# Scheduler inputs, batch 1's mask, output buffers and a rounded layout changed in a fused attention and FFN kernel

## The chip, the cores and the metric

One core of one Trainium2 chip runs the program. The metric is device time in microseconds (us), the median over several executions. Engines are named as the profile names them: PE is TensorE's matmul, PEld its weight load, DVE is VectorE, ACT is ScalarE, POOL is GpSimd, SP is SyncE.

## The reference

Attention over 8 batches and 8 heads of 576 positions with 64 dimensions: heads 0 to 3 look at the last 32 positions, heads 4 to 7 at every fourth position of the last 128. Its output, laid out as 4608 tokens of 512, goes through a multiplicative feed-forward layer without a nonlinearity.

```python
scores = scale * np.matmul(q, k.transpose(0, 1, 3, 2))
mask_plain = (rel >= 0) & (rel < 32)
mask_dil = (rel >= 0) & (rel < 128) & (rel % 4 == 0)
scores = np.where(masks, scores, -1e9)
attn = np.exp(scores - max); attn = attn / attn.sum()
x = np.matmul(attn, v)               # (8, 8, 576, 64) -> (4608, 512)
a = x @ w1                           # w1, w2: 512 x 1024
b = x @ w2
h = a * b @ w3                       # w3: 1024 x 1024
out = h @ w_out                      # w_out: 1024 x 512
```

## The kernel before

**Attention.** In each batch, `u` = 0 is the four plain heads and `u` = 1 the four dilated ones, whose positions are taken residue by residue, so that both kinds need only a band of 128 keys for a block of 96 queries. A batch has 12 blocks (two `u` times six). q, k and v arrive by cast DMAs issued by GpSimd (`load_rows` L251, `load_v_plain` L288, `load_v_dil` L297); q and k of the very first half batch come unrounded over SyncE's queue into a staging area that is later `gt` (`load_whole` L260), and ScalarE rounds them in halves (`round_rows` L267). VectorE transposes q and k (`turn`, L401 and L416). A `Group` takes some blocks through scores (L467), the exponential on ScalarE (L478) and the mask. There are two ways to mask: in the first `BIASED` batches, groups hold three blocks and TensorE first adds a bias of -30000 outside the band by a product with the identity (L450); in the others groups hold `GRP` = 5 blocks, running on from batch to batch, and VectorE multiplies the exponentials by 0 or 1 (L486). That mask is made by five GpSimd instructions (L380), at the place that `MASK_AT` gives among GpSimd's DMAs. A `Step` is three blocks: the product with v and a column of ones (L509), reciprocal (L520) and normalisation (L523) on VectorE, and the transposition into `XT`: in the first two batches by TensorE (L537) with a copy out of PSUM by ScalarE (L545) or VectorE (L547), later by a DMA transpose on SyncE (L550). For the first two batches v's plain half is turned on TensorE too (L425, copies L435 and L437). `XT0` holds the plain heads, `XT1` the dilated ones.

**Feed-forward.** w3 and w_out are multiplied once into `wf_sb`: w3 is loaded (L336), transposed by VectorE (L659), multiplied with `wo_sb` (L679) and copied (L690 on ScalarE, L692 on VectorE). Tokens go in 16 units of 288, two per batch. `up` (L574) makes the products with w1 and w2, four matmuls for each 128 columns: two that read `XT1`, two that read `XT0`. ScalarE copies the first product (`copy_a` L585) and VectorE multiplies (`gate` L589) into `gt`. `down` (L600) multiplies tiles of 128 tokens with `wf_sb`; ScalarE copies the result into a buffer `osb` (L611), of which there are three, and SyncE stores it (L650). The last tile goes in two halves (`down_part` L618, `finish` L627), whose three pieces are copied into one `osb` tile.

**The order.** No hardware queue decides the order: `Plan` (L58 on) takes every step as a task with an engine, an assumed duration, dependencies and a priority, simulates the five engines, PSUM's eight banks and the stream of DMAs, and emits instructions in the order that comes out; each engine then runs its own list in that order, and real dependencies become semaphore waits. Priorities come from `FIRST` (batch 0) and `RANK` (others), the order of the first loads from `FIRST_LOADS`. `ON_DVE` names copies that VectorE does instead of ScalarE, `HALVED` those that both share. `SINGLE` is the number of products at the start that are made one 128-column piece at a time rather than two; `PARTED` is how many products of the first unit may be split into a part for the plain and one for the dilated heads. Where a load is issued the plan assumes (issue, transfer) times, and `BUSY` is added where a SyncE transpose is issued while the DMA stream is occupied. Where PE would idle before the first product, the plan inserts warming matmuls (L724; 25 more stand at the very start, L704).

Of the kernel before, what the change touches and what calls it, by code (L numbers as in the profile page):

```python
# [10 lines left out]
P = 128  # L11
BF16 = mybir.dt.bfloat16
# [17 lines left out]
BIASED = 2  # L30
LATE = False
W3_DVE = (0, 1, 2, 3)
SINGLE = 10
# [4 lines left out]
RANK = dict(E=14.678, VK=10.289, K=0.115, N=1.309, T=1.47, VT=1.262, S=3.624, V=0.444, X=8.99, W=0.183, C=2.862)  # L38
FIRST = dict(E=3.06, VK=0.542, K=2.149, N=1.723, T=5.596, VT=64.744, S=0.678, V=0.475, X=11.212)
WARM = 25  # L40
FILL = 110
FIRST_LOADS = ('k01', 'v00', 'q01', 'd0', 'v10', 'w0', 'w1', 'q10', 'k10', 'w2', 'q11', 'k11', 'd1', 'o0', 'o1', '33', '32', '31', '30')
SHIFT = {}
ON_DVE = ('VK0.0.1', 'VK0.1.1', 'VK1.0.0', 'VK1.1.0', 'W3D5', 'W3D6')
# [3 lines left out]
HALVED = ('K0.2', 'K0.3', 'VK0.1.0', 'VK0.1.1', 'VK1.0.0', 'VK1.1.0')  # L48
MASK_AT = 31.5
PARTED = 0  # L50
BUSY = 4500
# [14 lines left out]
class Plan:  # L66
# [15 lines left out]
    def run(self):  # L82
# [42 lines left out]
        while len(order) < n:  # L125
            progress = True
            while progress:
                progress = False
                for e in engines:
# [22 lines left out]
                    if e == "DMA":  # L152
                        free[e] = now + t.dur[0]
                        if t.dur[1]:
                            if len(landed) >= 8:
                                free[e] = max(now, landed[-8]) + t.dur[0]
                            dma = max(dma, free[e]) + t.dur[1]
                            t.end = dma + 1900
                            landed.append(t.end)
                        else:  # L160
                            t.end = free[e]
                    else:
                        t.end = free[e] = now + t.dur
                        if e == "SP" and t.name[0] == "X" and dma > now:
                            t.end = free[e] = now + t.dur + BUSY
                            dma += 1.5 * t.dur
# [23 lines left out]
def kernel(  # L190
# [60 lines left out]
    def load_rows(nm, src, b, us):  # L251
        if (nm, b) not in qk:
            qk[(nm, b)] = qk_pool.tile([P, 2, 18 * D], BF16, tag=nm, name=nm)
# [6 lines left out]
    def load_whole(nm, src, u):  # L260

        at = {"qn": 0, "kn": 18 * D, "vn": 36 * D}[nm]
# [4 lines left out]
    def round_rows(nm, u, half):  # L267

        at = {"qn": 0, "kn": 18 * D, "vn": 36 * D}[nm]
        if (nm, 0) not in qk:  # L270
            qk[(nm, 0)] = qk_pool.tile([P, 2, 18 * D], BF16, tag=nm, name=nm)
        o, i = qk[(nm, 0)][:, u, :], stage[:, at : at + 18 * D]
        if nm == "qn":
            n, c0 = ((5, 0), (4, 2 * D))[half]
            o, i = (
                bass.AP(tensor=x.tensor, offset=x.offset + c0, ap=[x.ap[0], [4 * D, n], [1, 2 * D]])
                for x in (o, i)
            )
        else:
            c = slice(9 * D * half, 9 * D * half + 9 * D)  # L280
            o, i = o[:, c], i[:, c]
        nc.scalar.copy(out=o, in_=i)  # L282
# [107 lines left out]
    def turn(b, u, nm, part):  # L390
# [6 lines left out]
        if part in (None, 6, 7):  # L397
# [5 lines left out]
        n, first, odd = ((5, 0, RUN + 4), (4, RUN, 5 - RUN))[part % 2]  # L403
        low = max(0, part // 2 - 1)
# [8 lines left out]
            offset=src.offset + (part % 2) * 64 + low * 32,  # L413
            ap=[src.ap[0], [128, n], [32, both], [1, 32]],
# [194 lines left out]
    def copy_y(i):  # L609
        o_sb = wk_pool.tile([P, d_model], F32, tag="osb", bufs=3, name="osb")  # L610
# [16 lines left out]
    def finish(i, half):  # L627

        if half == 0:
            held[("o", i)] = wk_pool.tile([P, d_model], F32, tag="osb", bufs=3, name="osb")  # L630
        o_sb = held[("o", i)]
# [4 lines left out]
        nc.vector.tensor_copy(out=o_sb[:, c0 : c0 + n], in_=held[("y", i, half)][:, 0:n])  # L636
        nc.sync.dma_start(out=rows[:, c0 : c0 + n], in_=o_sb[:, c0 : c0 + n])
        if half == 1:
            nc.scalar.copy(out=o_sb[:, c0 + n :], in_=held[("y", i, half)][:, n:])
            nc.scalar.dma_start(out=rows[:, c0 + n :], in_=o_sb[:, c0 + n :])  # L640
# [102 lines left out]
    def loads_rows(nm, b, us=None):  # L743
# [4 lines left out]
        t = load(f"L{nm}{b}", 700, 3100 if us is None else 1600, old,  # L748
# [4 lines left out]
    def loads_v(b):  # L753
        old = vdone.get((b - 2, 0), [])
        LV[(b, 0)] = [load(f"LP{b}", 1300, 4700, old, lambda: load_v_plain(b))]

    def loads_vd(b):
        old = vdone.get((b - 2, 1), [])
        LV[(b, 1)] = [
            load(f"LD{b}.{i}", 600, (800, 670, 400, 1070)[i], old, lambda i=i: load_v_dil(b, i))  # L760
# [5 lines left out]
    def loads_w12(c):  # L766
        return [
            load("LW", 800, (1700, 1700, 3300)[c], [], lambda d=d, s=s: load_w(d, s, WC[c]))
# [3 lines left out]
    for i, nm in enumerate(WHOLE):  # L772
        t = add(f"LF{nm}", "SP", 100, [], lambda nm=nm: load_whole(nm, rows_of[nm], 0), -9 + i,
                lat=4400 + 1350 * i)
        L[(nm, 0, 0)] = [
            add(f"C{nm}.{half}", "ACT", 650, [t], lambda nm=nm, h=half: round_rows(nm, 0, h),
                -9 + i + 0.1 * half, lat=100)
# [15 lines left out]
    for x in FIRST_LOADS:  # L793
# [3 lines left out]
        elif x[0] == "o":  # L797
            lwo[c] = load(f"LWO{c}", 600, 3300, [], lambda c=c: load_wo(c))
        elif x[0] == "3":
            n, move = (4, 700) if c in W3_DVE else (2, 1400)  # L800
# [38 lines left out]
    def turns(b, u, nm, pr):  # L839
# [4 lines left out]
        else:  # L844
            parts = (2, 3, 4, 5) if b == 0 else (0, 1)
# [16 lines left out]
    for b in range(B):  # L862
# [10 lines left out]
        if b < DIRECT_V:  # L873
            tv = turns(b, 0, "vn", 10 * b + rank("T", b))
            for half in range(2):
                x = add(f"VT{b}.0.{half}", "PE", 420, tv[half] + [idt],
# [61 lines left out]
        while steps < 4 * B:  # L938
# [21 lines left out]
            if bb < TURNED:  # L960
                x = add("X" + n, "PE", 310, ns + [idt], st.back, bb - 99 + rank("X", bb), slot=1)
# [10 lines left out]
            else:  # L972
                x = [add("XD" + n, "SP", 1300, ns, st.back_dma, 0, lat=1200)]
# [39 lines left out]
    def downs(i):  # L1013
# [4 lines left out]
        if i == n_y - 1:  # L1018
            for half in range(2):
# [3 lines left out]
                    after=stores[-3:-2])  # L1023
# [4 lines left out]
                 after=[stores[-3] if len(stores) > 2 else None])  # L1028
        stores.append(add("ST", "SP", 300, [cy], lambda: store(i), 0, lat=3000))
# [61 lines left out]
```

## Time and profile before

| | us |
|---|---|
| device time, four runs | 254.45, 255.04, 256.07, 257.23 |
| median | 255.55 |
| the profiled execution | 255.04 |
| its span | 253.3 |
| TensorE busy | 242.7 |
| VectorE busy | 158.5 |
| ScalarE busy | 109.5 |
| GpSimd busy | 62.4 |

How to read the rows: a group's row names the line, engine, operation, output <- input, shape and count, then the busy time, the mean in ns of one instruction, and the idle time in front of the group with what ended it. A timeline row has start, length, engine, line and, in brackets, the idle time before it. Matmuls overlap in the pipeline, so the price of one is read from the distance of starts, not from the mean length. In the page's slices each digit is tenths busy in a fortieth of the span. The rows that matter are shown with the prediction.

### The profile page before, as it was taken

What the parts mean: (1) busy time and instruction counts of PE and PEld (TensorE: products, weight loads), DVE (VectorE), ACT (ScalarE), POOL (GpSimd) and SP (SyncE); (2) the same over time, 40 slices, a digit from 0 to 9 for tenths busy, and PEclk for the clock granted to TensorE, in tenths of its full rate; (3) what the DMA queues carried; (4) which work ended last, traced back from release to release, by engine and by line L of the source; (5) the groups of instructions that cost most, each with busy time, mean ns of one, the idle gap of its engine ahead of it and who ended that gap; (6) DMA issues with size and microseconds to landing.
All of it is one profiled execution on the core that took longest, in us unless ns stands there. A gap on an engine that the chain in (4) does not pass through costs nothing.

```text
span 253.3 us, 6390 instructions
## 1 busy us (share of the span) xinstructions
PE 242.7 (96%) x2694; PEld 167.1 (66%) x2694; DVE 158.5 (63%) x270; ACT 109.5 (43%) x154; POOL 62.4 (25%) x96
## 2 busy tenths in 40 slices
PE   7799999999996999999999999999999999999994
PEld 5488677646555657667677676776766766777752
DVE  3988575879776797888488591974545543232221
ACT  5655555225513354452544523553535524323321
POOL 7754479378212223133002110300000000000000
PEclk9999999999999999999999999999999999999999
DMA  7999999999999999999994929294161631221114
GB/s 225 197 200 205 203 203 144 159 192 189 184 210 162 217 206 242 150 102 173 168 172 52 145 51 135 84 117 92 43 91 41 67 91 41 70 73 49 44 41 124
DMA packets 58749, 33.90 MB, mean 134 GB/s; under 512 B 42081, under 2 KB 49633, under 8 KB 58721
## 3 DMA queue, kind: packets, MB, share of 16 engines
q0 software_dynamic: 37920, 19.34, 60.0%
q1 hardware_dynamic: 20656, 14.10, 29.6%
q8 instruction: 21, 0.34, 0.6%
q10 hardware_dynamic: 144, 0.07, 0.1%
q14 instruction: 8, 0.06, 0.1%
HBM read 39.85 MB, written 9.44 MB: 195 GB/s over the span
## 4 chain that ended last, share of the span: by engine, by line
PE 77%; DMA 18%; ACT 1%; issue 1%; POOL 0%; DVE 0%; SPq 0%; ACTq 0%; POOLq 0%; DVEq 0%
PE ps L574 44%; PE ps L600 21%; PE ps L679 5%; DMA kn<-in_k_dram 5%; DMA out_dram<-osb 4%; PE ps L509 3%; DMA w_sb<-in_moe_w_dram 3%; PE ps L467 3%; DMA w3n<-in_moe_w_dram 3%; DMA vn<-in_v_dram 3%; ACT et L478 1%; PE ps L618 1%; DVE et L486 0%; ACT asb L585 0%; ACT osb L611 0%
## 5 line engine op out<-in xcount | busy, mean ns | idle before, releaser
L574 PE MATMUL ps<-XT,w_sb 128*128 128x288 bf16 x1024 | 135.9, 286 | 0.2 <-ACT asb L585 0.2
L574 PEld LDWEIGHTS <-w_sb 128*128 128x128 bf16 x1024 | 97.9, 98 | 30.5 <-issue 0.2
L589 DVE TENSOR_TENSOR gt<-ps,asb 128x576 bf16<-128x576 f32 (+1 forms) x69 | 49.2, 713 | 62.4 <-PE ps L574 56.6
L585 ACT CAST asb<-ps 128x576 bf16<-128x576 f32 (+1 forms) x69 | 41.7, 605 | 66.9 <-PE ps L574 65.2
L600 PE MATMUL ps<-wf_sb,gt 128*128 128x512 bf16 x280 | 65.7, 379 | 0.0
L600 PEld LDWEIGHTS <-gt 128*128 128x128 bf16 x280 | 27.0, 98 | 26.9
L611 ACT COPY osb<-ps 128x512 f32<-128x512 f32 x35 | 20.4, 587 | 51.0 <-PE ps L600 48.0
L478 ACT ACTIVATE et<-ps 128x1920 bf16<-128x1920 f32 (+2 forms) x23 | 34.4, 1510 | 5.6 <-PE ps L467 5.6
L301 POOL DMA_DIRECT2D vd<-in_v_dram x32 | 21.3, 671 | 48.8 <-PE ps L509 43.7
L523 DVE TENSOR_TENSOR xo<-ps,rcp 96x768 bf16<-96x768 f32 x32 | 30.1, 949 | 0.7
L416 DVE STREAM_TRANSPOSE qt<-qn 128x320 uint32<-128x320 uint32 (+3 forms) x34 | 22.2, 674 | 2.1 <-ACT qn L282 1.7
L486 DVE TENSOR_TENSOR et<-et,mask 128x960 bf16<-128x960 bf16 (+1 forms) x30 | 17.7, 630 | 0.3 <-ACT et L478 0.2
L509 PEld LDWEIGHTS <-et 128*128 128x128 bf16 x384 | 14.2, 98 | 2.9 <-ACT et L478 1.6
L467 PE MATMUL ps<-qt,kt 32*128 32x96 bf16 x768 | 12.5, 201 | 3.5 <-ACT osb L611 2.1
L520 DVE RECIPROCAL rcp<-ps 96x12 f32<-96x12 f32 x32 | 6.7, 217 | 14.5 <-PE ps L509 14.4
L467 PEld LDWEIGHTS <-kt 32*128 32x128 bf16 x768 | 9.2, 92 | 9.2 <-issue 7.2
L679 PE MATMUL ps<-wo_sb,w3T 128*128 128x512 bf16 x64 | 14.1, 379 | 0.0
L416 DVE STREAM_TRANSPOSE kt<-kn 128x320 uint32<-128x320 uint32 (+3 forms) x18 | 11.4, 641 | 2.5 <-PE ps L467 2.3
L290 POOL DMA_DIRECT2D vp<-in_v_dram x6 | 7.2, 1200 | 22.1 <-PE ps L509 16.1
L336 POOL DMA_DIRECT2D w3n<-in_moe_w_dram x16 | 9.3, 585 | 7.7 <-DVE w3T L659 4.3
L679 PEld LDWEIGHTS <-w3T 128*128 128x128 bf16 x64 | 6.3, 98 | 7.2
L401 DVE STREAM_TRANSPOSE kt<-kn 128x576 uint32<-128x576 uint32 (+1 forms) x9 | 10.0, 1123 | 0.5 <-PE ps L467 0.5
(56 smaller groups left out, 112.7 us busy)
## 6 DMA issues: line engine op xcount, KB each, us to landing
qn<-in_q_dram POOLq DMA_DIRECT2D x6, 576.0 KB, 9.6
kn<-in_k_dram POOLq DMA_DIRECT2D x6, 576.0 KB, 11.4
w3n<-in_moe_w_dram POOLq DMA_DIRECT2D x16, 128.0 KB, 6.6
out_dram<-osb SPq DMA_DIRECT2D x7, 256.0 KB, 2.3
out_dram<-osb SPq DMA_DIRECT2D x8, 224.0 KB, 3.4
vp<-in_v_dram POOLq DMA_DIRECT2D x6, 288.0 KB, 11.1
out_dram<-osb SPq DMA_DIRECT2D x8, 192.0 KB, 2.3
out_dram<-osb SPq DMA_DIRECT2D x8, 160.0 KB, 2.7
```

The lines of the kernel that those rows point to most:

```text
L301: nc.gpsimd.dma_start(out=vds[b % 2][p0 : p0 + n, :, mu, 16 : 16 + 2 * D], in_=v_rows(b, 4, 4 * t0 + res, [[4 * D, n], [S * D, 4], [1, 2 * ...
L416: nc.vector.transpose(out=o, in_=i)
L467: nc.tensor.matmul(out=self.sp[:, g, QB * i : QB * i + QB], lhsT=kt[prt, u, QB * m : QB * m + P, c], rhs=qq, start=(c == 0 and not biased) ...
L478: nc.scalar.activation(out=ev, in_=self.sp[:, :, 0:x], func=ACT.Exp, scale=scale)
L509: nc.tensor.matmul(out=self.o[:, g, mm, :], lhsT=grp.et[:, c0 : c0 + P], rhs=vv, start=True, stop=True,)
L523: nc.vector.tensor_tensor(out=self.xo[0:QB, :].rearrange("p (m g d) -> p g m d", m=3, g=4), in0=self.o[0:QB, :, :, self.val : self.val + D ...
L574: nc.tensor.matmul(out=o[:, i, :], lhsT={"a": w1_sb, "b": w2_sb}[key][:, c, f * P : (f + 1) * P], rhs=unit_cols(k, c), start=(first and j ...
L585: nc.scalar.copy(out=held[("s", k, fs[0])], in_=held[("a", k, fs[0])])
L589: nc.vector.tensor_tensor(out=gt[:, fs[0] : fs[-1] + 1, c0 : c0 + UNIT], in0=held[("b", k, fs[0])], in1=held[("s", k, fs[0])], op=AL.mult,)
L600: nc.tensor.matmul(out=y, lhsT=gt[:, f, c0 : c0 + P], rhs=wf_sb[:, f, :], start=(f == 0), stop=(f == KFF - 1),)
L611: nc.scalar.copy(out=o_sb, in_=held[("y", i)])
L679: nc.tensor.matmul(out=o, lhsT=w3T[ft][:, g // 2, :, g % 2] if ft // 2 in W3_DVE else w3T[ft][:, g, :], rhs=wo_sb[:, g, :], start=(g == 0) ...
```

## The change

The plan's assumed times for transfers, transposes and stores are replaced by others, with a different rule for SyncE while DMA is busy, and the priorities, load order and assignment of copies are other numbers; with these the plan gives another order on every engine. `BIASED` falls from 2 to 1, so batch 1's blocks join the groups of five that VectorE masks, and the last of these groups with blocks of batch 1 runs on into batch 2. `MASK_AT` puts the mask's five instructions ahead of all loads that are still to be issued. `SINGLE` = -132 makes every product two pieces wide, `PARTED` = 80 lets all products of unit 0 be parted. `osb` has six buffers, and the last tile's three pieces get a buffer each. The first q's rounded halves are stored one behind the other instead of interleaved, and `turn` reads them so; v's tile for rows holds one half batch.

```diff
-BIASED = 2
+BIASED = 1
+OSB = 6
+QUARTERS = ('qn', 'kn')
-SINGLE = 10
+SINGLE = -132
-RANK = dict(E=14.678, VK=10.289, K=0.115, N=1.309, T=1.47, VT=1.262, S=3.624, V=0.444, X=8.99, W=0.183, C=2.862)
-FIRST = dict(E=3.06, VK=0.542, K=2.149, N=1.723, T=5.596, VT=64.744, S=0.678, V=0.475, X=11.212)
+RANK = dict(E=0.351, VK=60.432, K=24.778, N=0.18, T=72.284, VT=18.559, S=28.466, V=10.21, X=6.94, W=1.028, C=33.53)
+FIRST = dict(E=0.125, VK=3.069, K=21.212, N=0.305, T=7.654, VT=0.231, S=160.797, V=2.276, X=20.076)
-FIRST_LOADS = ('k01', 'v00', 'q01', 'd0', 'v10', 'w0', 'w1', 'q10', 'k10', 'w2', 'q11', 'k11', 'd1', 'o0', 'o1', '33', '32', '31', '30')
+FIRST_LOADS = ('v00', 'k01', 'q01', 'q10', 'v10', 'd0', 'w1', 'w0', 'k10', 'q11', 'k11', 'w2', 'd1', 'o0', '32', 'o1', '31', '30', '33')
-ON_DVE = ('VK0.0.1', 'VK0.1.1', 'VK1.0.0', 'VK1.1.0', 'W3D5', 'W3D6')
+ON_DVE = ('K0.0', 'K0.2', 'K0.3', 'K1.0', 'K1.1', 'K1.2', 'VK1.1.0', 'VK1.1.1', 'W3D3', 'W3D5', 'W3D7')
-HALVED = ('K0.2', 'K0.3', 'VK0.1.0', 'VK0.1.1', 'VK1.0.0', 'VK1.1.0')
-MASK_AT = 31.5
-PARTED = 0
-BUSY = 4500
+HALVED = ('K0.2', 'K1.0', 'K1.3', 'VK1.0.1', 'VK1.1.0', 'VK1.1.1')
+MASK_AT = -61.5
+PARTED = 80
+BUSY = 7500
...
-                        if e == "SP" and t.name[0] == "X" and dma > now:
-                            t.end = free[e] = now + t.dur + BUSY
-                            dma += 1.5 * t.dur
+                        if e == "SP" and now > 20000 and dma > now:
+                            t.end += min(BUSY, dma - now)
+                            dma += (1.5 if t.name[0] == "X" else 1) * t.dur
...
-        o, i = qk[(nm, 0)][:, u, :], stage[:, at : at + 18 * D]
+        o, i = qk[(nm, 0)][:, 0, :], stage[:, at : at + 18 * D]
         if nm == "qn":
             n, c0 = ((5, 0), (4, 2 * D))[half]
-            o, i = (
-                bass.AP(tensor=x.tensor, offset=x.offset + c0, ap=[x.ap[0], [4 * D, n], [1, 2 * D]])
-                for x in (o, i)
+            i = bass.AP(
+                tensor=i.tensor, offset=i.offset + c0, ap=[i.ap[0], [4 * D, n], [1, 2 * D]]
             )
+            o = o[:, 10 * D * half : 10 * D * half + n * 2 * D]
+            nc.scalar.copy(out=o.rearrange("p (n x) -> p n x", n=n), in_=i)
...
+        pitch, at = (64, 320) if (b, u, nm) == (0, 0, "qn") and nm in WHOLE else (128, 64)
...
-            offset=src.offset + (part % 2) * 64 + low * 32,
-            ap=[src.ap[0], [128, n], [32, both], [1, 32]],
+            offset=src.offset + (part % 2) * at + low * 32,
+            ap=[src.ap[0], [pitch, n], [32, both], [1, 32]],
...
-        o_sb = wk_pool.tile([P, d_model], F32, tag="osb", bufs=3, name="osb")
+        o_sb = wk_pool.tile([P, d_model], F32, tag="osb", bufs=OSB, name="osb")
...
-        if half == 0:
-            held[("o", i)] = wk_pool.tile([P, d_model], F32, tag="osb", bufs=3, name="osb")
-        o_sb = held[("o", i)]
...
-        nc.vector.tensor_copy(out=o_sb[:, c0 : c0 + n], in_=held[("y", i, half)][:, 0:n])
-        nc.sync.dma_start(out=rows[:, c0 : c0 + n], in_=o_sb[:, c0 : c0 + n])
+        y = held[("y", i, half)]
+        o_sb = wk_pool.tile([P, d_model], F32, tag="osb", bufs=OSB, name="osb")
+        nc.vector.tensor_copy(out=o_sb[:, 0:n], in_=y[:, 0:n])
+        nc.sync.dma_start(out=rows[:, c0 : c0 + n], in_=o_sb[:, 0:n])
         if half == 1:
-            nc.scalar.copy(out=o_sb[:, c0 + n :], in_=held[("y", i, half)][:, n:])
-            nc.scalar.dma_start(out=rows[:, c0 + n :], in_=o_sb[:, c0 + n :])
+            o2 = wk_pool.tile([P, d_model], F32, tag="osb", bufs=OSB, name="osb")
+            nc.scalar.copy(out=o2[:, 0:n], in_=y[:, n:])
+            nc.scalar.dma_start(out=rows[:, c0 + n :], in_=o2[:, 0:n])
...
-        t = load(f"L{nm}{b}", 700, 3100 if us is None else 1600, old,
+        t = load(f"L{nm}{b}", 700, 2850 if us is None else 1450, old,
...
-        LV[(b, 0)] = [load(f"LP{b}", 1300, 4700, old, lambda: load_v_plain(b))]
+        LV[(b, 0)] = [load(f"LP{b}", 1300, 1900, old, lambda: load_v_plain(b))]
...
-                x = [add("XD" + n, "SP", 1300, ns, st.back_dma, 0, lat=1200)]
+                x = [add("XD" + n, "SP", 1700, ns, st.back_dma, 0, lat=1200)]
...
-                 after=[stores[-3] if len(stores) > 2 else None])
-        stores.append(add("ST", "SP", 300, [cy], lambda: store(i), 0, lat=3000))
+                 after=[stores[-OSB] if len(stores) >= OSB else None])
+        stores.append(add("ST", "SP", 900, [cy], lambda: store(i), 0, lat=1500))
```

The other assumed times change in the same way (weights 1700 to 1400 and 3300 to 2580, w_out 3300 to 2500, w3 700 to 680, v's dilated parts, roundings, turns back).

## The prediction

> **What bounds the kernel now.** I read the page first, then the chain of waits in order of time, then TensorE's own timeline, then the groups of instructions by shape and the timelines of VectorE and GpSimd around the places that the change touches.
>
> ```profile
> PE 242.7 (96%) x2694; PEld 167.1 (66%) x2694; DVE 158.5 (63%) x270; ACT 109.5 (43%) x154; POOL 62.4 (25%) x96
> ...
> PE   7799999999996999999999999999999999999994
> ...
> PEclk9999999999999999999999999999999999999999
> DMA  7999999999999999999994929294161631221114
> ```
>
> TensorE is busy for 96% of the span at full granted clock; the only thin spots are the first slices and one after 75 us. The DMA engines are saturated for the first half.
>
> ```profile
> 43.04 4.90 PE ps L574 x40
> 47.94 10.36 PE ps L679 x48
> ...
> 69.98 10.28 DMA out_dram<-osb
> 80.34 0.59 ACT osb L611
> 80.98 0.61 PE ps L467 x40
> ...
> 247.82 1.76 PE ps L618 x16
> ```
>
> This is the chain of waits (start, length, what). From 43.04 on it is one TensorE matmul after another, with one excursion: a store of the output (10.28 us from issue to landing, at 69.98) releases ScalarE's copy out of PSUM at 80.34, and that releases score matmuls at 80.98. So a microsecond of TensorE work or waiting is a microsecond of time.
>
> ```profile
> 18.86 0.50 PE L425 MATMUL ps<-ident,vt 128*128 128x128 bf16 x6
> 19.19 1.63 PE L574 MATMUL ps<-XT,w_sb 128*128 128x288 bf16 x12
> ...
> 42.87 5.07 PE L574 MATMUL ps<-XT,w_sb 128*128 128x288 bf16 x40
> ...
> 80.98 0.61 PE L467 MATMUL ps<-qt,kt 32*128 32x96 bf16 x40 [2.06 <-ACT osb L611]
> ```
>
> TensorE's own timeline (start, length, line, shape, count, idle before): the first w1/w2 product (L574) starts at 19.19, and the store costs 2.06 us of idle time.
>
> The time as a sum. The steps between chain rows give a price for one matmul: L574 0.1225 us (4.90/40), 512 columns 0.2158 (10.36/48), a score 0.014 (0.56/40), L509 0.0305 (0.73/24), L537 0.045 (0.26/6), L425 0.06, L618 0.11. With the page's counts: 1024 L574 125.4, 280 L600 60.4, 64 L679 13.8, 16 L618 1.8, 384 L509 11.7, 768 L467 10.7, 32 L450 3.9, 48 L537 2.2, 24 L425 1.4: 231.3 us of work. At 43.04 the work ahead of it in the queue adds up to 28.8, so 14.2 had gone to waiting and warming matmuls. From there to 249.58 pass 206.5 us for 202.5 of work: 4.0 lost, 2.2 of it at the store, the rest some 0.1 after each score group. The tail to 253.30 is 3.7. 14.2 + 231.3 + 4.0 + 3.7 = 253.2, the span. The profiled execution took 255.04, 1.74 more than its span; the median of the runs shown is 255.55, 0.5 above it.
>
> **The change part by part.**
>
> ```profile
> L486 DVE TENSOR_TENSOR et<-et,mask 128x960 bf16<-128x960 bf16 x28 | 17.1, 650 | 0.3 <-ACT et L478 0.2
> ...
> L450 PE MATMUL ps<-bias,ident 128*128 128x288 bf16 x32 | 5.3, 287 | 0.0
> ```
>
> *Batch 1 masked by VectorE.* Its four groups of three blocks lose their 16 bias matmuls (L450): 16 x 0.1225 = 1.96 us of TensorE work, and the built order has 21 score groups instead of 23, 0.1 each: **-2.1 us**. VectorE's order gains four multiplications of 0.650 us, two of 768 columns (0.348 to 0.650, I take 0.53) and loses two of 0.348: +3.0 us. VectorE is busy 39.8 of the first 55 us, and has gaps of 2.7 us at 27, 36.6 and 43, so I cost that at nothing on the path; without that cover it is at most 3.0. ScalarE's exponentials stay (8 x 1.128 + 14 x 1.777 + 0.816 against 4 x 1.128 + 16 x 1.777 + about 1.46, 34.7 and 34.4).
>
> *Six osb buffers.* The copy at 80.34 is the fourth; its product was done at 75.8, and it waited for the first store, landed at 80.26. With six buffers that store is needed by the seventh copy, which this trace has at 92.7: **-2.2 us**. Bound: 0 if something else holds ScalarE there; nothing else is named. In the final tile each part has a buffer of its own:
>
> ```profile
> 249.60 0.29 DVE L636 COPY osb<-ps 128x128 f32<-128x128 f32 x1 [0.45 <-PE ps L618]
> 249.97 0.27 ACT L639 COPY osb<-ps 128x128 f32<-128x128 f32 x1 [1.49 <-DVE osb L636]
> ```
>
> In these rows of the end ScalarE's last copy waits for VectorE's copy into the same tile, though its product ended at 249.58: it starts 0.35 earlier, and its transfer is the last issued: **-0.3 us** (0 to -0.35).
>
> *First q's rounded halves apart.*
>
> ```profile
> 6.08 1.46 DVE L416 STREAM_TRANSPOSE qt<-qn 128x320 uint32<-128x320 uint32 x2 [1.75 <-ACT qn L282]
> 7.40 1.23 DVE L401 STREAM_TRANSPOSE kt<-kn 128x288 uint32<-128x288 uint32 x2
> ```
>
> VectorE's first transposition waits for both roundings on ScalarE (4.81 + 0.725 + 0.612, overlapping, end 6.05). Apart, it starts after the first, at 5.6. Of the 0.45 us nothing reaches the scores, because of the next part.
>
> *The order.* This is the large unknown. VectorE's queue now has v's transposition (1.24 us) and two of k's quarter pieces ahead of the second half of the first k. GpSimd issues v before k now; the first two such loads landed at 7.54 and 9.0, so k's quarters wait for 9.0. The queue: q 5.6 to 6.95, half of k to 7.6, v to 8.85, quarters 9.05 to 9.85, k's other half to 10.5. The first scores start at 10.6 instead of 8.68. Behind them VectorE still has six quarters and batch 1's first q (to 13.5), then two steps of reciprocal and normalisation at 0.22 + 0.95 less overlap (15.75), a copy of XT (576 wide; 288 took 0.308, so 0.31 to 0.62, I take 0.46), half a q and batch 1's v (17.95), two more steps (20.2). L540 turns the last, and the first L577 starts at **20.6**, where 19.19 was. The four w1/w2 quarters must have landed: two of them now go behind batch 1's q (1.4 us), all behind the masks.
>
> ```profile
> 35.79 4.76 POOL L380 TENSOR_SCALAR mask<-bias 128x384 bf16<-128x384 bf16 x5
> ```
>
> GpSimd's five mask instructions, 4.76 us, stood at 35.79 and now stand at about 5.1, in front of v, vd and the weights. This is covered by the transfers already queued: landings follow each other by 1.3 to 1.5 us per 288 KB (7.54, 9.0, 10.35), so the two loads of q end at 11.8, and a load issued at 9.85 lands 3.9 later (0.57 of issue, then about the 3.0 of the quickest w3n load, and half a us for its size), 13.7 instead of 13.2. Then vd (2.2 us, from its landings), weights at 1.2 each: 17.0, 18.2, 19.4, 20.7, just in time. [...]
>
> From the first L577 to the point where both first units are done (128 of them) there are 18.7 us of work in the new order; before, 21.8 took 23.85. I follow the queue: a short wait for the gate in front of batch 1's scores (0.3), one for normalisation in front of the first turn back (0.5), 0.2 for the rest, that is 40.3. As before lost 2.05 there, I take 1.7: **41.0**. Bounds: 39.7 (waits of 0.4) and 44 (kn and qn of batch 1, by the same steps at 22.1 and 23.5, each 1.5 late, and the second w_out load, at 39.4, after the 40 us at which the fused weights need it).
>
> In the new order 26.0 us of work lie ahead of that point (28.8 less 1.96 of bias, 0.86 for 16 scores, 12 L509 and 6 L537 that now come later), so 15.0 are lost there against 14.2: **+0.8 us**. From there 229.3 - 26.0 = 203.4 us of work remain and 1.8 of small losses: TensorE ends at 246.2. The mask's old place costs nothing any more: q and k of batch 2 landed at 52.1 and 54.8, now some 4.5 earlier. Tail 3.4, outside the span 1.74: **251.35 on the profiled execution, 3.7 less (the parts, -2.1 - 2.2 - 0.3 + 0.8, give 3.8); on the median 251.8.** Of the rest (larger PSUM-to-SBUF copies by VectorE instead of ScalarE, double units from the start, eight fused-weight copies shared 3 to 5) each moves below a microsecond between engines with gaps, and I cost it at 0.
>
> **The rivals.**
> 1. *The masks aren't covered.* If the queue runs dry for most of the 4.76 us, weights and batch 1's k land up to 3 us later, and the first unit and all behind it with them: 254 to 255. For it: the four weights land without margin. Against: landings that follow the transfers by 1.4 us each show a backlog until 11.8.
> 2. *Slower: batch 1's last scores hang on batch 2's loads.* Its third group holds two blocks of batch 1 and three of batch 2, so TensorE, which takes its queue in order, stands there (at about 54) until batch 2's q and k have landed and been transposed (1.3 us after k). I have k at 50.4, margin 2. If it lands at 52.6 it begins to cost, one for one; the gain is gone at 56.3, and over 1% is lost from 58.9 on: 259. Before, it landed at 54.8 behind the masks, so it needs four microseconds worse than that.
> 3. *The store's wait only moves.* VectorE's later transpositions or batch 2's DMA transposes (up to 12 us to landing at 75 to 100, needed at about 87, issued at about 76) end in its place: 2.2 come back, 254.
>
> **How the numbers follow.** Forecast 0.60, rival 1 0.15, rival 3 0.13, rival 2 0.12. About 1% is what a measurement of this kernel tells from no change, 253.0 and 258.1. The forecast lies below 253.0 almost whole (0.58 of 0.60), and a few of the rivals 1 and 3 do (0.03); rival 2 is slower by over 1% in most of its 0.12. Faster 0.61, same 0.28, slower 0.11. The forecast's own range, from the bounds 39.7 and 42.5, is 250.3 to 253.3; with rivals 1 and 3 taken in, and 0.7 below for the small losses, 249.6 to 255.5.
>
> **What would show it.** L450 falls to 16 and the idle time before scores around 80 is gone; ScalarE's osb copies wait only for TensorE; the first L577 at 20.6 and the first L682 at 41; TensorE's end near 246; the last ScalarE copy starts with its product's end. Wrong would be a wait in front of L682 or the scores at 54 named after a DMA, w_sb named in front of the first L577, or score groups at 85 to 90 that wait for XT.

## The result and the profile after

The kernel after takes **256.06 us** (median of 53 runs, 253.6 to 261.95), the kernel before 254.49 (79 runs, beside them): ratio **1.0035, 95% interval 1.0021 to 1.005**. The ratio leaves out the executions in a second, slower state (12 of the 53), which the median of 256.06 contains. It is slower by 0.9 us on that ratio, where 3.7 less was forecast. The profiled execution took 255.45 with a span of 253.7.

The page of the kernel after: busy time by engine, then TensorE's 40 slices, its granted clock and the bytes moved.

```profile
PE 243.7 (96%) x2687; PEld 167.1 (66%) x2687; DVE 162.8 (64%) x274; ACT 106.2 (42%) x143; POOL 62.3 (25%) x96
...
PE   7895999999999999999999999999999999999994
...
PEclk9997999999999999999999999999999999999999
...
GB/s 226 183 141 204 202 199 200 188 169 187 197 161 214 196 158 216 227 220 179 112 125 83 84 136 78 151 44 65 90 44 90 44 65 90 46 70 52 41 44 124
```

A slice is 6.3 us. The hole after 75 us is gone; a new one is in the fourth slice, 19 to 25 us, where the granted clock sinks too, and the transfers run at 141 GB/s in the slice before it. The chain of waits (start, length, what) says what it is:

```profile
5.07 4.77 POOL mask L382 x5
10.36 2.66 POOL vd L303 x4
13.02 2.19 POOL w_sb L313 x3
15.21 9.19 DMA w_sb<-in_moe_w_dram
24.44 3.98 PE ps L577 x24
```

The end hangs on GpSimd's masks, on the issues of v's dilated loads and of the weights behind them, and on the fourth weight load, which took 9.19 us from issue to landing. The store at 69.98 and ScalarE's copy at 80.34 have left the chain. TensorE's timeline around it:

```profile
20.16 0.43 PE L540 MATMUL ps<-ident,xo 96*128 96x96 bf16 x6
23.23 5.67 PE L577 MATMUL ps<-XT,w_sb 128*128 128x288 bf16 x32 [2.63 <-DMA w_sb<-in_moe_w_dram]
...
44.77 3.62 PE L682 MATMUL ps<-wo_sb,w3T 128*128 128x512 bf16 x16
```

TensorE is through with the work ahead of the first up product at 20.59, as forecast (20.6). It then waits 2.63 us for weights, 32 products take 5.67 us, and the first fused-weight product starts at 44.77 instead of 41.0. From there to TensorE's end at 250.0 are 205.2 us, exactly the forecast's 203.4 + 1.8. So against the forecast 3.8 us are lost ahead of 44.77 and nothing behind it, up to TensorE's end.

The windows of the kernel after (stretch; busy time of the engines; then granted clock, DMA share, GB/s):

```profile
10.00:12.00 2.00, 2.00 (x56) 1.32 (x58) 1.93 (x6) 1.63 (x3) 2.00 (x4) 1.00 0.84 128
12.00:14.00 2.00, 1.74 (x54) 1.51 (x40) 1.92 (x6) 1.46 (x2) 2.00 (x4) 1.00 1.28 175
14.00:16.00 2.00, 1.41 (x41) 0.94 (x38) 1.97 (x5) 0.93 (x1) 2.00 (x4) 1.00 1.41 133
16.00:18.00 2.00, 2.00 (x52) 1.61 (x52) 1.96 (x4) 1.15 (x2) 2.00 (x4) 1.00 1.13 129
18.00:20.00 2.00, 2.00 (x38) 1.77 (x34) 1.87 (x3) 2.00 (x5) 0.78 (x2) 1.00 1.31 168
```

GpSimd (the fifth busy column) is occupied without a pause to 18, yet the transfers run at 128 to 175 GB/s, where the kernel before has 188 to 213 in these stretches. The four weight loads land at 19.3, 20.7, 23.2 and 24.4.

Theory A: GpSimd issues nothing for 4.77 us while it makes masks, the stream of transfers thins, and the weights come 3.7 us late (the prediction's rival 1). Rivals: the new order of the loads, or their mix, is the cause, whatever GpSimd does (B and F below); or the sunken clock is. In most of the experiments the plan's order is kept and only named tasks are emitted elsewhere, behind `order, _ = plan.run()`. Every ratio is to the kernel before, run beside it.

### The profile page after: what moved, and what is told of

Read it like the earlier page. It is cut to its first block, busy times and chain, and to the rows that moved or that the text cites. A ratio compares the mean times of both kernels' runs of the same rounds, so it can differ in the third digit from the quotient of the medians.

```text
span 253.7 us, 6352 instructions
## 1 busy us (share of the span) xinstructions
PE 243.7 (96%) x2687; PEld 167.1 (66%) x2687; DVE 162.8 (64%) x274; ACT 106.2 (42%) x143; POOL 62.3 (25%) x96
## 4 chain that ended last, share of the span: by engine, by line
PE 88%; POOL 5%; DMA 4%; DVE 1%; issue 1%; ACT 0%; POOLq 0%; ACTq 0%
PE ps L577 50%; PE ps L603 24%; PE ps L682 5%; PE ps L512 4%; PE ps L470 4%; DMA w_sb<-in_moe_w_dram 4%; POOL mask L382 2%; POOL vd L303 1%; POOL w_sb L313 1%; PE ps L621 1%; PE ps L540 0%; POOL qn L258 0%; POOL vn L258 0%; DVE xo L526 0%; ACT asb L588 0%
## 5 line engine op out<-in xcount | busy, mean ns | idle before, releaser
L577 PE MATMUL ps<-XT,w_sb 128*128 128x288 bf16 x1024 | 138.3, 288 | 2.9 <-DMA w_sb<-in_moe_w_dram 2.6
L592 DVE TENSOR_TENSOR gt<-ps,asb 128x576 bf16<-128x576 f32 x64 | 48.3, 754 | 59.9 <-PE ps L577 58.9
L588 ACT CAST asb<-ps 128x576 bf16<-128x576 f32 x64 | 40.9, 639 | 69.3 <-PE ps L577 67.8
L489 DVE TENSOR_TENSOR et<-et,mask 128x960 bf16<-128x960 bf16 (+1 forms) x34 | 20.5, 645 | 0.2 <-ACT et L481 0.2
```

Source lines behind the costliest of these rows:

```text
L489: nc.vector.tensor_tensor(out=ev, in0=ev, in1=mk, op=AL.mult)
L577: nc.tensor.matmul(out=o[:, i, :], lhsT={"a": w1_sb, "b": w2_sb}[key][:, c, f * P : (f + 1) * P], rhs=unit_cols(k, c), start=(first and j ...
L588: nc.scalar.copy(out=held[("s", k, fs[0])], in_=held[("a", k, fs[0])])
L592: nc.vector.tensor_tensor(out=gt[:, fs[0] : fs[-1] + 1, c0 : c0 + UNIT], in0=held[("b", k, fs[0])], in1=held[("s", k, fs[0])], op=AL.mult,)
```

## Experiments: where the masks stand

**Masks behind the four weight loads.** The kernel after, and:

```diff
     order, _ = plan.run()
+    moved = [t for t in order if t.name.startswith("masks")]
+    order = [t for t in order if not t.name.startswith("masks")]
+    at = [i for i, t in enumerate(order) if t.name == "LW"]
+    at = at[3] + 1
+    order[at:at] = moved
```

> The changed kernel, every list as it is but GpSimd's: the five mask instructions go behind the issue of the first four weight loads (w1 and w2, columns 0 to 511). Theory A (the masks keep GpSimd from issuing, the DMA stream runs thin from 10 to 18 us, and the weights land 3.7 us late): the fourth weight lands near 20.7 instead of 24.4, the first L577 starts at 20.2 to 20.7, the granted clock stays at 1.0 between 22 and 26 us, L682 starts near 41.5 instead of 44.77, and the time falls by 3 to 3.5 us, to some 252. Theory B (this mix of loads moves at 130 to 175 GB/s whoever issues it): the weights still land after 23, the time stays within 1 us of 255.5. Theory C (a wait at batch 1's scores takes its place, because batch 1's k is issued at 16 either way): the first product starts at 20.6, but the time falls by less than 2 us, with an idle time of over 1 us in front of the first scores of batch 1.

Measured: 254.14, ratio 0.9971 (0.9947 to 0.9995). Its TensorE timeline:

```profile
20.37 4.19 PE L577 MATMUL ps<-XT,w_sb 128*128 128x288 bf16 x32
...
40.85 3.62 PE L682 MATMUL ps<-wo_sb,w3T 128*128 128x512 bf16 x15
...
58.15 3.63 PE L682 MATMUL ps<-wo_sb,w3T 128*128 128x512 bf16 x15 [1.68 <-DVE w3T L662]
```

The wait for weights is gone and the fused weights start 3.9 earlier, as theory A says. But the masks (now at 14.18) hold up the loads behind them: the transfers fall to 138 GB/s at 20 to 22, VectorE waits for w3, and TensorE 1.68 for it at 58.15. TensorE ends at 248.68, 1.3 before the kernel after: 2.6 of the 3.9 are given back.

**Masks behind batch 1's k.** The same edit with `"Lkn1"` and `[1]`: three more loads go first.

> The same, with the masks one step further, behind batch 1's k and q as well, where GpSimd only waited for transfers. Theory A: the gain of the run before, and batch 1's k lands near 22 instead of 25.8, so no wait in front of batch 1's scores: 3.5 to 4.5 us faster than the changed kernel, 251 to 252. Theory B: within 1 us of 255.5. Theory C: this run, other than the one before it, brings the whole gain. If the masks come late for VectorE's first multiplication of batch 1 (at 28 to 30 us), an idle time of VectorE in front of L489 shows it; I expect none, as they end near 18.

Measured: **252.73, ratio 0.9915 (0.9887 to 0.9943)**. Masks at 15.86; the transfers stay at 195 to 213 GB/s from 14 to 26.

```profile
40.68 3.62 PE L682 MATMUL ps<-wo_sb,w3T 128*128 128x512 bf16 x15
...
56.00 3.63 PE L682 MATMUL ps<-wo_sb,w3T 128*128 128x512 bf16 x15 [0.23 <-DVE w3T L662]
...
89.15 5.07 PE L577 MATMUL ps<-XT,w_sb 128*128 128x288 bf16 x40 [0.73 <-DMA XT<-xo]
```

One move of five instructions is worth 3.3 us on the medians, and the kernel is then faster than both. The 0.73 at 89.15 is the prediction's rival 3 in small: a DMA transposition comes too late.

**The converse: masks early in the kernel before.** The same loop, its insertion point ahead of the first `LD0` load. The masks are then made from the bias tile before its blocks are filled, so later batches are multiplied by other masks.

> The kernel before, with its own order, in which only the five mask instructions of GpSimd are emitted earlier, ahead of the first dilated load of v, as in the kernel after. Theory A (masks in front of the loads thin the stream of transfers and delay the first weights): the weights, which land at 15.8, 17.0, 18.6 and 19.7 in the kernel before, land 3 to 4.5 us later, at 19 to 24; the DMA rate at 10 to 18 us falls from about 200 GB/s to 130 to 180; the first fused-weight matmul (L679) comes 2 to 4 us after 43.04; the time rises by 1.5 to 4 us, to a ratio of 1.006 to 1.016. Rival B (the order of the loads of the kernel after is what costs, not the masks): weights within 1 us of before, time within 0.7 us of before.

Measured: 258.33, ratio 1.0145 (1.0096 to 1.0194). (The 43.04 quoted there is the start of the 40 up products ahead of the fused weights; their first, L679, stands at 47.77 in the kernel before.)

```profile
23.39 1.63 PE L574 MATMUL ps<-XT,w_sb 128*128 128x288 bf16 x12
...
51.98 4.26 PE L679 MATMUL ps<-wo_sb,w3T 128*128 128x512 bf16 x19
...
84.10 0.61 PE L467 MATMUL ps<-qt,kt 32*128 32x96 bf16 x40 [0.99 <-ACT osb L611]
```

The first up product, 19.19 before, and the first fused weight both come 4.2 later; the wait for the store, 2.06 before, shrinks to 0.99, as TensorE arrives later. 4.2 - 1.07 = 3.1 is the growth of the span, 253.3 to 256.4.

The weights do come late: GpSimd's next issues, which wait for the four of them, start at 19.40, 21.40, 22.99 and 24.02 instead of 16.08, 17.30, 18.91 and 19.94, and the transfers run at 75 to 155 GB/s from 10 to 18. But this is not what makes the time. Here the masks read the bias tile ahead of VectorE's last write to it, so that write waits for them, and with it the first transposition (6.08 before). VectorE's timeline, then TensorE's first scores (8.68 before):

```profile
9.40 0.22 DVE L373 MEMSET bias<- 32x192 bf16 x1 [6.25 <-POOL mask L380]
9.55 1.38 DVE L416 STREAM_TRANSPOSE qt<-qn 128x320 uint32<-128x320 uint32 x2
```

```profile
12.07 0.67 PE L467 MATMUL ps<-qt,kt 32*128 32x96 bf16 x24 [1.75 <-DVE kt L401]
```

The write stands at 4.12 in the kernel before. 3.4 of the 4.2 are lost by the first scores, the rest while the granted clock is 0.53 and 0.62 (12 to 16), and at 23.39 TensorE waits for no weight. So the old order shows the late landings of theory A, but its time decides nothing between A and B. The next run does.

**Masks on VectorE.** The kernel after, its order untouched:

```diff
-        nc.gpsimd.tensor_scalar(
+        nc.vector.tensor_scalar(
```

> The kernel after with its order unchanged, in which the five mask instructions run on VectorE, where they stand between the last bias fill (to 4.36) and the first transposition (5.62, which waits for ScalarE), and GpSimd has no mask at all. Theory A (GpSimd's 4.76 us of masks in front of the loads is the whole fault): the second load of v is issued at 5.0, the four weights land between 15 and 20 (19.3 to 24.4 in the kernel after), the first up product starts at 20.2 to 20.6 without a later stop, the first fused-weight matmul at 40.5 to 41; and as GpSimd makes no masks later either, the later loads and the transposes of XT come no later than in masks_behind_k, so the time is that of masks_behind_k or up to 0.8 less: 251.9 to 252.7, ratio 0.989 to 0.9925. VectorE's masks take 0.9 to 1.4 us, and if they run past 5.62 the first scores move by that (0 to 0.3 us). Rival F (the order of the loads is at fault as well): weights later than 21, time 254 or more.

Measured: 253.27 (6 runs, 251.97 to 258.38), ratio 0.9926 (0.988 to 0.9972). The masks take 0.2 us each there; the first transposition starts at 5.65 instead of 5.62, the first up product at 20.48 without a stop, the first fused weight at 40.57. Rivals B and F fall: in the same order of the same loads the weights are in time if GpSimd only issues. The execution profiled was the longest of the six, so only its start is read here; what stopped it is taken up below.

## Experiments: what else the weights' delay could be

**The two weight halves exchanged.**

```diff
+    at = [i for i, t in enumerate(order) if t.name == "LW"][:4]
+    lw = [order[i] for i in at]
+    for i, t in zip(at, lw[2:] + lw[:2]):
+        order[i] = t
```

> The changed kernel with the two pairs of weight loads exchanged: the columns 0 to 255 that the first products read are loaded before 256 to 511; the masks stay in front. Theory A and B alike: the first pair lands at 19.3 and 20.7, so the first L577 starts at 20.6, and TensorE waits for the second pair (24.4) after 12 matmuls instead of for the first after none: 1 to 1.5 us faster, 254 to 254.5. If the lateness were no matter of the weights, no change.

Measured: 255.15, ratio 1.0012 (0.9977 to 1.0046). The wait at 23.19 shrinks to 0.38 and the first fused weight starts at 42.11, 2.66 earlier. But the stream is as thin as before (130 to 140 GB/s in three of the four stretches from 10 to 18), so the later loads stay late: waits of 1.25 for w3 at 58.79 and 0.51 for XT at 92.28 follow, and TensorE ends at 250.35, no sooner than in the kernel after: in this execution the gain at the start is given back. On the medians 0.9 of it is left (255.15 against 256.06), but the intervals of the two ratios overlap.

**The clock.** 32 warming matmuls (`fill()`) ahead of the first up product.

> The changed kernel with 32 more warming matmuls (3.4 us) in front of the first L577, where TensorE waits for the weights (20.6 to 24.4). It tells what of the loss is the clock that fell to 0.5 to 0.7 after the idle time: if the lowered clock adds its own time behind the wait, the 24 matmuls that took 3.98 us take 2.94 and the time falls by about 1 us; if the transfers alone set the pace there, nothing changes.

Measured: 256.22, ratio 1.0036 (1.0004 to 1.0067). The clock stays at 1.00, 32 products take 4.08 instead of 5.67, the first fused weight comes 0.86 earlier, TensorE ends at 249.66 (0.34 earlier) and the median doesn't move. In all ten runs the granted clock averages 0.997 or more, in over half of those of the kernel after 0.993 or less, and the time is no shorter for it. So the clock is a consequence and costs next to nothing here.

**The dilated loads behind the weights.** `LD0` tasks moved behind the fourth `LW`, masks left in front.

> The kernel after, masks where they are on GpSimd, in which only the four dilated loads of v's first batch (352 KB in short pieces, some 0.67 us of GpSimd each) are issued behind the first four weight loads instead of ahead of them. It asks why the stream ran at some 130 GB/s from 10 to 18 us, as long as 8 us after the masks. Theory G (the issuing is what the stream waits for: each load that is ahead costs GpSimd its issue time): the weights are issued 2.66 us earlier and land 1.5 to 2.7 us earlier, last at 21.7 to 22.9, and the rate at 10 to 18 stays near 140. Rival H (the short pieces of the dilated loads, with nothing long beside them, thin the stream): the rate at 12 to 18 rises to about 200 GB/s and the last weight lands at 19.5 to 21. In both the first product of the dilated half comes later (it needs these loads), so the total is no measure here.

One execution: 259.68; the dilated half waits for its v at 21.25, so the total says nothing, as expected. GpSimd's next issues, which wait for the four weights, start at 16.82, 18.18, 19.50 and 20.98 instead of 19.58, 20.93, 23.46 and 24.68: the last lands 3.7 earlier, at 20.7. From 10 to 16 the rate is 135, 162 and 105 GB/s, and 193 from 16 on. That is neither theory as written: the landing is H's, the thin rate up to 16, without any short pieces, is G's. So v's dilated loads, which stand between the masks and the weights, have a part in the delay. What brings the stream back to 200 GB/s stays open; that it takes some 6 us from GpSimd's first issue is all that is shown.

## Experiments: the other terms of the sum

**Six buffers alone.** The kernel before with `bufs=6` for osb, order unchanged (v's unused half tiles halved, for room).

> The kernel before, with six osb buffers in place of three and its order unchanged (the tiles of v, of which only one half is used, are halved to make room). The prediction's second term: the copy at 80.34 no longer waits for the first store, the 2.06 us of idle TensorE at 80.98 are gone, the end of TensorE comes 2.0 to 2.2 us earlier (247.4 in place of 249.58), ratio 0.991 to 0.993. Rival C (the wait only moves, to the transposing transfers of XT, which stand in the same queue as the stores, or to a load): the copies run on, but TensorE waits for XT or a weight between 80 and 100, and at most 1 us is gained, ratio 0.996 to 1.

Measured: **252.89 (12 runs), ratio 0.9925 (0.9894 to 0.9955)**. ScalarE's timeline of its osb copies:

```profile
73.34 0.59 ACT L611 COPY osb<-ps 128x512 f32<-128x512 f32 x1 [1.88 <-PE ps L600]
77.60 0.59 ACT L611 COPY osb<-ps 128x512 f32<-128x512 f32 x1
82.34 0.59 ACT L611 COPY osb<-ps 128x512 f32<-128x512 f32 x1 [0.99 <-PE ps L600]
```

The fourth copy stands at 77.60 instead of 80.34 and waits for no store; TensorE ends at 247.46, 2.1 before 249.58. The term was right, and nothing took the wait's place. This one change makes the kernel before as fast as masks_behind_k; their intervals overlap.

**Three buffers in the repaired kernel.** masks_behind_k with `bufs=3`.

> The kernel masks_behind_k with three osb buffers in place of six, order unchanged: it puts back one part of the change alone. Prediction's second term: the fourth copy waits for the first store again, TensorE loses about 2.2 us near 78 to 82, ratio to before 1.000 against 0.9915. Rival C (the wait would only be exchanged with that for XT, 0.73 + 1.2 us at 89): the loss is 1 us or less, ratio 0.993 to 0.996.

Measured: 254.86 (253.15 to 259.99), ratio 0.9989 (0.9958 to 1.0019). The loss has about the forecast's size, but not its place:

```profile
75.87 0.58 ACT L614 COPY osb<-ps 128x512 f32<-128x512 f32 x1 [2.06 <-PE ps L603]
...
248.51 0.27 ACT L642 COPY osb<-ps 128x128 f32<-128x128 f32 x1 [2.73 <-DMA out_dram<-osb]
```

No copy near 80 waits for a store: the new order spreads the first copies, so that the fourth stands at 75.87, 12 us behind the first (in the kernel before the first three lie within 4 us). The wait is at the very end, where the last tile takes three buffers; the span ends 4.84 after TensorE instead of 3.7. This profile is 0.8 above that of masks_behind_k, the median 2.1; the other 1.3 is not explained.

**The bias matmuls put back.** masks_behind_k, batch 1 biased too:

```diff
+            n1 = sum(x[0] == 1 for x in self.blocks)
+            for g in range(4 if n1 else 0):
+                nc.tensor.matmul(
+                    out=self.sp[:, g, 0 : n1 * QB],
+                    lhsT=ident,
+                    rhs=mask[:, 0:n1, :],
+                    start=True,
+                    stop=False,
+                )
...
```

> The kernel masks_behind_k in which batch 1's three score groups are biased as well as masked: 12 more matmuls on TensorE (480, 480 and 192 columns, four of each), together the 4,608 columns of the 16 that the change removed; what they add is 0 or 1, the same factor for all kept weights of a row or close to it for the purpose of the time, so its output isn't the reference's. Prediction's first term (a microsecond of TensorE work is one of time): 4,608 columns at 0.2158 per 512 are 1.94 us, TensorE's end 1.9 later than 247.22, total 1.6 to 2.0 more (254.3 to 254.7), ratio 0.9975 to 1.000. Rival K (near the start, where TensorE still waits for loads, the matmuls lie in waiting time): 0 to 1.0 more, ratio 0.9915 to 0.9955.

Measured: 253.86, ratio 0.9978 (0.9962 to 0.9995), 1.1 above masks_behind_k. TensorE's timeline:

```profile
26.17 0.97 PE L462 MATMUL ps<-mask,ident 128*128 128x480 bf16 x4
...
30.68 0.97 PE L462 MATMUL ps<-mask,ident 128*128 128x480 bf16 x4
...
42.45 3.62 PE L691 MATMUL ps<-wo_sb,w3T 128*128 128x512 bf16 x15
```

At the fused weights the kernel is 1.77 later (42.45 against 40.68): the eight matmuls of 480 columns that stand ahead of them are 1.62 by the price of the term, and a wait of 0.17 for a weight is new. The four of 192 columns follow at 55.75. TensorE's end is only 1.04 later, where the term has 1.94: the waits for w3 and XT at 56 and 89, 0.23 and 0.73, are gone, as the loads had more time. Both theories hold for a part: the term is right where the matmuls stand, and about half of it lies in time that was waited for transfers further on.

**The mask alone, planned anew.** six_osb with `BIASED = 1` and the masks on VectorE.

> The kernel six_osb (252.89) with batch 1 masked instead of biased, its order planned anew by the scheduler of the kernel before, and the masks on VectorE at its idle start, so that no GpSimd time is spent on them: the prediction's first term by itself. 16 bias matmuls of 0.1225 and two score groups fewer: 2.1 us less work of TensorE, so 250.8 if nothing waits, ratio 0.984 to 0.987. Rival 2 of the prediction (batch 1's last scores share a group with batch 2's and wait for batch 2's loads, or the new order loses it): 252.5 to 256, with a wait of TensorE for batch 2's q or k before 70.

Measured: 264.93 (260.39 to 266.25). The scheduler made another order of everything. TensorE waits 1.98 at 30.14 for VectorE's masked exponentials and 2.7 in three pieces from 43 to 46, the fused weights start at 49.74 instead of 47.77, and 4.85 are lost to an XT transposition at 98.41. It has no wait for batch 2's q or k, and with all else changed it gives no price for the term.

**Two banks at the end.** masks_behind_k; the last 256 columns as two products into two PSUM banks.

```diff
...
+            for o, w0 in ((y[:, 0:n], 2 * n), (ps[:, at, 0:n], 3 * n)):
...
```

> The kernel masks_behind_k, in which the last 256 columns of the last tile are made as two products of 128 columns (16 matmuls in place of 8) into two PSUM banks, so that the last copies of VectorE and ScalarE read different banks; their output tiles are apart already. Theory D (ScalarE's last copy waited for VectorE's because both read one bank): ScalarE's copy L649 names TensorE as what it waited for, both copies lie side by side, the last store is issued 0.3 earlier, less some 0.1 for the eight more matmuls: the time between the end of TensorE and the end of the span falls from 3.7 to 3.4, total 0.1 to 0.3 less than masks_behind_k. Rival E (the order between the engines has another reason): ScalarE still waits for VectorE, tail 3.7, and total 0 to 0.2 more than masks_behind_k.

Measured: 252.96, ratio 0.9931 (0.9897 to 0.9965). ScalarE's last copy first in the kernel after, then with two banks:

```profile
250.39 0.27 ACT L642 COPY osb<-ps 128x128 f32<-128x128 f32 x1 [1.53 <-DVE osb L638]
```

```profile
247.33 0.27 ACT L656 COPY osb<-ps 128x128 f32<-128x128 f32 x1 [1.18 <-PE ps L625]
```

With tiles apart but one bank it waits for VectorE's copy, so the shared tile was not the reason. With two banks it waits for TensorE's product. The name of the last wait alone would not settle it, since VectorE's copy ends before that product here (at 247.18, against 247.30). But ScalarE passes both semaphore waits in front of the copy by 245.6, while with one bank (masks_behind_k) the second of them lasts 2.02 us, until VectorE is done. So the shared bank made the order here, as theory D says. But the tail stays 3.7: ScalarE's store is issued at 247.63 instead of 247.91 (masks_behind_k) and takes 2.1 to land instead of 1.7, so it lands no sooner.

**A copy that waits in front of work.** The profiled execution of v_masks, 258.38, was stopped here:

```profile
87.89 0.48 DVE L310 COPY vp<-vp 32x1280 bf16<-32x1280 bf16 x1 [6.69 <-DMA vp<-in_v_dram]
88.41 1.23 DVE L489 TENSOR_TENSOR et<-et,mask 128x960 bf16<-128x960 bf16 x2
```

The new order puts the halo copy HALO4, which waits for a load, in front of batch 3's masks. That load took 16.24 us (in the kernel after some 10, with a wait of 0.65), and TensorE stood 5.07. In two kernels, made from the kernel after and from v_masks, the copy is emitted behind the task `M3.2.0.1`; in halo_later it then stands at 101.52, 9 us ahead of its reader at 110.77.

> The kernel after, in which only VectorE's halo copy of v's fifth batch (HALO4, L310), which stands at 85.74 right in front of the masks of batch 3 although its own reader V4.0 comes 20 us later, is emitted behind the masks of batch 3's third step. Theory I (the new order puts a copy that waits for a transfer, at the very time that the transfer is planned to land, in front of work that TensorE needs; in some executions the transfer is later and everything behind it stops): no wait of VectorE for vp near 82 to 88; the time falls by what it cost on average, 0.3 to 1.5 us (254.6 to 255.8), and runs lie closer together than the 253.6 to 262 of the kernel after. Rival J (the wait of 0.65 there costs nothing): 255.8 to 256.3, spread as before. The late weights stay in both: the first fused-weight matmul near 44.8.

> The kernel v_masks with the same later halo copy. Theory I: its stop of 5.07 us at 89.12 cannot occur, median 251.5 to 252.3, ratio 0.988 to 0.9905, and runs closer together than 251.97 to 258.38. Rival J: median 252.7 to 253.5 as in v_masks. In either case the first up product at 20.5, the first fused-weight matmul at 40.6, and a wait for XT (90 to 98) is what may come next.

Measured: 255.45 for the first, ratio 1.0029 (1.0002 to 1.0055), and 252.62 for the second, ratio **0.9911 (0.9891 to 0.9931)**, 251.76 to 253.13. Both medians are 0.6 lower than without the edit, but the intervals overlap, and the first still has a run at 260.81. That this copy costs something in the common run is not shown, nor why the runs of the kernel after lie further apart than those of the kernel before.

## Why the prediction was wrong

The step that failed is "This is covered by the transfers already queued", with what it led to: "weights at 1.2 each: 17.0, 18.2, 19.4, 20.7, just in time". The cover was counted to the first load behind the masks, and there it was right: v landed at 13.9 (forecast 13.7). But the backlog was used up by then. Behind v came eight loads up to the last weight, each issued some 0.7 after the one before, and the stream ran at 128 to 175 GB/s instead of some 200. v's four dilated loads and the first weight took 5.4 us behind v, to 19.3 (forecast 3.3, to 17.0); the other three weights took 5.1 (forecast 3.7), and the last came 3.7 late. The 2.2 for the dilated loads and the 1.2 for a weight were the spacing of a full queue, taken over to a thin one. The four weight loads of 256 KB, several in flight, took 6.3 to 9.2 us each from issue to landing. Rival 1 is what happened; its chance was 0.15, and its price of "up to 3 us" was 0.7 too low.

The forecast's own range was also drawn too narrow from its own bounds: it ends at 253.3 by a first fused weight at 42.5, while the bound worked out above it is 44. With 44 it would have ended at 254.8, still below the measured median.

The other steps:

- **Order up to the first up product.** First scores at 10.81 (10.6), the work ahead of the first up product done at 20.59 (20.6). Right.
- **First fused weight at 41.0.** 40.68 and 40.57 where the weights are not late; 44.77 as built, beyond the upper bound of 44.
- **From there 203.4 + 1.8 us.** 205.2. Right as built. With the start mended (masks_behind_k) it is 206.5, from 40.68 to 247.22, as TensorE then waits at 56 and 89; so 251.35 would not have been reached there either.
- **Batch 1 masked, -2.1.** L453 has 16 matmuls left. Put back, 1.94 of matmuls cost 1.04 at the end of the repaired kernel: right in kind, half in size once transfers decide.
- **Six buffers, -2.2.** 2.1 alone in the old order. In the new order three buffers would not have waited at 80; what six save there is at the tail.
- **Tail tiles apart, -0.3.** 0: with the tiles apart ScalarE's copy still waited 1.53 for VectorE's; with two banks it did not, and the store's landing, 2.1 instead of 1.7, took the gain.
- **First q's halves.** VectorE starts at 5.62 (5.6); nothing reaches the scores. Right.
- **Rival 2.** No wait of TensorE for batch 2's loads near 54. **Rival 3:** no wait for XT in the kernel after; 0.73 at 89.15 once the start is mended.

3.8 at the start and 0.3 at the tail make the 4.1 between 251.35 and the profiled 255.45; the median is 0.6 above that execution, where 0.5 was allowed.

## What to carry to other kernels

Before an issuing engine is given several microseconds of other work, count the loads in flight: in the kernel after they carried the stream to 10 (209 GB/s from 8 to 10), and from there it was thin to 20 (128 to 175), in vd_behind to 16 (105 to 162). The same five instructions cost 4.1 us at the first fused weight and 2.8 at TensorE's end behind four of GpSimd's loads (250.0 against 247.22), 1.5 at TensorE's end with the weights ahead of them too (248.68 against 247.22), and nothing that shows with three loads more, or on an engine that had gaps. A wait that is shortened by exchanging loads, without more bytes moved by then, can return at a later load: 2.63 for the weights became 0.38, and 1.25 for w3 followed. And an experiment that moves instructions can add a dependency of its own: see what the moved ones read, and look for a new wait before the time is put down to the theory.

## What the runs showed of the hardware

The granted clock sank after a short gap of TensorE. In the kernel after, whose last matmul ended at 20.59 (windows of 0.4 us, granted clock third from the end):

```profile
22.40:22.80 0.40, 0.00 (x0) 0.00 (x0) 0.00 (x0) 0.00 (x0) 0.00 (x0) 1.00 1.17 203
22.80:23.20 0.40, 0.00 (x0) 0.00 (x0) 0.00 (x0) 0.00 (x0) 0.00 (x0) 0.51 1.11 204
...
26.00:26.40 0.40, 0.40 (x4) 0.25 (x3) 0.40 (x1) 0.00 (x0) 0.28 (x1) 0.73 1.19 216
26.40:26.80 0.40, 0.40 (x6) 0.32 (x4) 0.40 (x1) 0.32 (x1) 0.40 (x1) 1.00 1.11 189
```

It halved after 2.2 us without a matmul and was back 3 us after the next one started (23.23); in vd_behind it halved 1.0 us after the last matmul, while in masks_first 2.7 us without one (6.95 to 9.67) passed at 1.00 (mean of 8 to 10). So one run's clock halved 1.0 us into a gap, and another's stood at 1.00 to the end of a gap of 2.7; what decides is not shown.

The five masks took 4.77 us on GpSimd; on VectorE they took 0.19 to 0.25 each.
